# The product with T of six chunks in seven half products instead of four whole ones

## The chip, the cores and the metric

The kernel runs on one core of one Trainium2 chip. The metric is the device time of one execution in microseconds, the median of repeated runs. The kernel is written instruction by instruction for the engines: PE (TensorE, matmuls and weight loads), ACT (ScalarE), DVE (VectorE), POOL (GpSimd) and SP, which here only issues DMAs.

## The reference

Attention with pooled queries, and then a multiplicative feed-forward block. Everything is float32 outside; the kernel works in float16 with float32 accumulation.

```python
# q, k, v: (8, 8, 1152, 64); w1, w2: (512, 1024); w3: (1024, 1024); w_out: (1024, 512)
q_pool = q.reshape(B, H, S // 2, 2, D).mean(axis=3)
scores = scale * np.matmul(q_pool, k.transpose(0, 1, 3, 2))
attn = softmax(scores)                       # over the keys
x = np.matmul(attn, v)                       # -> (4608, 512), tokens x (heads * D)
a = x @ w1
b = x @ w2
h = a * b @ w3
out = h @ w_out                              # (4608, 512)
```

## The kernel before

**Folding.** `w3 @ w_out` is one matrix T (1024 x 512), made once on PE (`t_groups`: transposes of w3, then products with w_out, L561) and kept as `T16`. What remains behind attention, for each chunk of 512 tokens, is: a = x w1 and b = x w2 (transposed, 1024 x 512), g = a * b, and out = g^T T.

**Attention.** The 8 x 8 heads are taken as 32 pairs of heads, four pairs to a batch. Scores are computed transposed, keys on the partitions, and cut into 324 slots of 512 columns; `scores` (L443, L448) makes two 512-column products into one of three PSUM buffers `psc`, and ACT's exp brings them to a ring in SBUF that holds 2.7 pairs. An attention group (`av_mm`, L474 or L471) multiplies 128 queries of a pair, or the 64-query rests of two pairs, with v; `av_norm` divides on DVE. There are 144 groups. The normalised x comes transposed into `xT` through PE for the first eight pairs and through a transposing DMA on SP (`x_dma`, L485) afterwards.

**Loading.** For each pair POOL casts k, sums pairs of q rows and casts v (`prepare`, `cast_kq`, `cast_v`: L355, L359, L361, L368), two pairs ahead; k and q are then transposed by PE (the first eight) or by a DMA on SP (`transp`, L375), one pair ahead. Loads are issued by SP (by POOL for the early pairs).

**Chunks.** There are nine chunks. Chunks 0 to 6 go through `moe_groups(c)`, a generator of steps that fill PE's time in the attention loop. A step names its cost, a function that issues matmuls into a PSUM bank, and a function that takes the result out. A chunk has 16 projection steps (for each of 8 row tiles `ft`, one with w1 whose result `keep` copies to `asb`, one with w2, L583, whose result `gate` multiplies by `asb` into `gT`, L614), each 4 x 512 columns, and then four steps that multiply 128 tokens each with T (L621, 8 x 512 columns, L630). Chunks 7 and 8 (`LATE` is 7) stand behind the loop in `late_chunks`, in an order written out by hand; there all three products go by seven half-size products instead of eight (the Strassen-Winograd scheme), with the sums of weights, of T and of x made on POOL (`weight_sums`, `x_sums`).

**Order.** A visit is three slots of scores and what the planner puts behind them; there are 108. `_visits` is a beam search over a small cost model (`_Plan`), run when the kernel is built. For each visit it chooses a sequence of attention groups ("A"), steps ("m" into the one bank `mo`, or "s" into one of the three `psc` buffers, then named `mot`) and PE transposes of k and q ("P"); DVE takes the results out of both kinds of bank. Steps run strictly in their order. A chunk's steps become available after a fixed number of groups (`loose`), and a group has an earliest visit (when the exps that it reads are done) and a latest one (when the ring is overwritten). Groups and steps that are left when the scores end are worked off in a tail.

**Queues.** Every engine executes its own instructions in program order. On POOL the casts, the sums and the issue of the output's stores stand in one queue; on SP the loads, the transposing DMAs and the stores of chunks 5 and 6.

Of the kernel before, what the change touches and what calls it, by code (L numbers as in the profile page):

```python
# [8 lines left out]
FP32 = mybir.dt.float32  # L9
# [174 lines left out]
def _visits(n, start, units, pairs, fills, free, ready, width):  # L184

    p = _Plan(7.0)
    for _ in range(3):  # L190
        p.scores(0.0)
    beam = {(0, 0): [p]}
    for vis in range(n):
        new = {}
        ats = pairs.get(vis, [])

        def end(p, seq, na, f):
            q = p.copy()
            for _ in range(3 if vis + 1 < n else 0):
                q.scores(ready[vis + 1])  # L200
            q.past = (p.past, seq)

            cost = q.lost() + 0.3 * max(q.av - q.t, 0.0) + 0.15 * max(q.mo - q.t, 0.0)
            new.setdefault((na, f), []).append((cost, seq, q))

        def step(p, seq, na, f, pr, t0):
            d = p.t - t0
            loose = free[na] if vis >= start else 0
            if pr == len(ats) and (na >= len(units) or units[na][3] > vis) and (d > 1.0 or f >= loose):
                end(p, seq, na, f)  # L210
            if d > 2.3 or len(seq) > 4:
                return
            if pr < len(ats):
                q = p.copy()
                q.pair(ats[pr])
                step(q, seq + "P", na, f, pr + 1, t0)
            if na < len(units) and units[na][2] <= vis and seq.count("A") < 3:
                q = p.copy()
                q.av_group(*units[na][:2])
                step(q, seq + "A", na + 1, f, pr, t0)  # L220
            if f < loose:
                for b in "ms":
# [43 lines left out]
def kernel(  # L266
# [277 lines left out]
    def t_groups():  # L544
        w3T = {}

        def turn(ft):
            def go(pt):
                w3T[ft] = msb.tile([128, NF, 128], FP16, tag="w3T", bufs=2, name="w3T")
                ph = pt.bitcast(FP16)  # L550
                for a in range(NF):
                    nc.tensor.transpose(ph[:, a * 128:a * 128 + 128],
                                        w3c[ft // 4][:, ft % 4, a * 128:a * 128 + 128], ident16)

            return 0.5, go, lambda pt: nc.vector.tensor_copy(out=w3T[ft].rearrange("p a i -> p (a i)"),
                                                             in_=pt.bitcast(FP16)), W3_AT[ft // 2]

        def mult(ft, n0):
            def go(pT):
                for a in range(NF):  # L560
                    nc.tensor.matmul(pT[:, 0:256], w3T[ft][:, a, :], wosb[:, a, n0:n0 + 256],  # L561
                                     start=(a == 0), stop=(a == NF - 1))

            return 1, go, lambda pT: nc.vector.tensor_copy(out=T16[:, ft, n0:n0 + 256], in_=pT[:, 0:256]), WO_AT

        for ft in range(0, NF, 2):
            yield turn(ft)
            yield turn(ft + 1)
            for n in range(4):
                yield mult(ft + n // 2, n % 2 * 256)  # L570

    CH = 512

    def runs(c):
        a = (c * CH) % XR
# [10 lines left out]
    def store(eng, pos, osb, cols=slice(0, dm), rows=slice(0, 128)):  # L586
# [7 lines left out]
            b, r = b + 1, r - QM * 128 - 2 * QT  # L594
        eng.dma_start(out=out[b * Sq:b * Sq + QM * 128, :].rearrange("(p c) n -> p c n", c=QM)[rows, r // 128, cols], in_=osb)  # L595

    def moe_groups(c):
        t = {}

        def first(pa, ft):  # L600
            if ft == 0:
                t["g"] = msb.tile([128, NF, CH], FP16, tag="g8", bufs=2, name="gT")
            proj(pa, w1sb, ft, c)

        def keep(pa):
            t["a"] = msb.tile([128, CH], FP32, tag="asb", bufs=2, name="asb")
            if tail[0]:
                nc.scalar.copy(out=t["a"], in_=pa)
            else:
                nc.vector.tensor_copy(out=t["a"], in_=pa)  # L610

        for ft in range(NF):
            def gate(pb, ft=ft):
                nc.vector.tensor_tensor(out=t["g"][:, ft, :], in0=pb, in1=t["a"], op=ALU.mult)  # L614

            yield 1, lambda pa, ft=ft: first(pa, ft), keep, 0.0
            yield 1, lambda pb, ft=ft: proj(pb, w2sb, ft, c), gate, 0.0
        for tt in range(0, CH, 128):
            def go(po, tt=tt):
                for ft in range(NF):  # L620
                    nc.tensor.matmul(po, t["g"][:, ft, tt:tt + 128], T16[:, ft, :],  # L621
                                     start=(ft == 0), stop=(ft == NF - 1))

            def put(po, tt=tt):
                osb = msb.tile([128, dm], FP32, tag="osb", bufs=3)
                if tail[0]:
                    nc.vector.tensor_scalar_mul(out=osb[:, 0:256], in0=po[:, 0:256], scalar1=1.0 / (SCL * SCL))
                    nc.scalar.mul(out=osb[:, 256:512], in_=po[:, 256:512], mul=1.0 / (SCL * SCL))
                else:
                    nc.vector.tensor_scalar_mul(out=osb, in0=po, scalar1=1.0 / (SCL * SCL))  # L630
# [10 lines left out]
    HF, HM, HC = NF // 2, dm // 2, CH // 2  # L641
    LATE = B * Sq // CH - 2
    IS = 1.0 / (SCL * SCL)
    wS, tS, xS = [], {}, {}

    def minus(out, x, y):
# [2 lines left out]
    def weight_sums():  # L649
        for w, tag in ((w1sb, "kst"), (w2sb, "vst")):  # L650
# [6 lines left out]
            minus(s3, a11, a21)  # L657
            minus(s4, a12, s2)
            wS.append({1: a11, 2: a12, 3: s4, 4: a22, 5: s1, 6: s2, 7: s3})
        b11, b12 = T16[:, 0:HF, 0:HM], T16[:, 0:HF, HM:dm]  # L660
        b21, b22 = T16[:, HF:NF, 0:HM], T16[:, HF:NF, HM:dm]
        st = [att.tile([128, 2, HF, HM], FP16, tag="qst", name="tS") for _ in range(2)]
        t1, t2, t3, t4 = st[0][:, 0], st[0][:, 1], st[1][:, 0], st[1][:, 1]
        minus(t1, b12, b11)
        minus(t2, b22, t1)
        minus(t3, b22, b12)
        minus(t4, b21, t2)
        tS.update({1: b11, 2: b21, 3: b22, 4: t4, 5: t1, 6: t2, 7: t3})

    def x_sums():  # L670
        st = msb.tile([128, 2, 4, NC // 2, HC], FP16, tag="wo", bufs=1, name="xS")
        for c in (0, 1):
            (_, a, n), = runs(LATE + c)
            b11, b12 = xT[:, 0:NC // 2, a:a + HC], xT[:, 0:NC // 2, a + HC:a + n]
            b21, b22 = xT[:, NC // 2:NC, a:a + HC], xT[:, NC // 2:NC, a + HC:a + n]
            x1, x2, x3, x4 = (st[:, c, i] for i in range(4))
            minus(x1, b12, b11)
            minus(x2, b22, x1)
            minus(x3, b22, b12)
# [151 lines left out]
    def fill(scored=False):  # L831
        if not head():
            return False
        n, go, put, at = ahead.pop(0)
        pt = bank(scored) if put else None
        go(pt)
        if put:
            put(pt)
        return True


# [14 lines left out]
        out=ident16, in_=ident16, compare_op=ALU.not_equal, fill=1.0,  # L856
        base=0, channel_multiplier=1, pattern=[[-1, 128]],
    )
    for _ in range(33):
        nc.tensor.matmul(avb[:, 0:64], ident16, ident16[:, 0:64], start=True, stop=True)  # L860
    for t in kq16s:
        nc.gpsimd.memset(t[QT:128, NB - 1], 0.0)
# [56 lines left out]
                      ((old * FLAT + RING + TO[t]) // G) // VS - 1))  # L919
    fills = []  # L920
    for ft in range(0, NF, 2):
        fills += [(0.5, W3_AT[ft // 2])] * 2 + [(1, WO_AT)] * 4
# [132 lines left out]
```

## Time and profile before

| | |
|---|---|
| median of 3 runs | 410.97 us (410.57 to 411.2) |
| the profiled execution's own time | 411.45 us |
| its span, first to last instruction | 409.8 us, granted clock 0.998 |
| PE busy | 396.8 us, 97% |
| ACT busy | 335.2 us, 82% |
| DVE busy | 218.7 us, 53% |
| POOL busy | 212.8 us, 52% |
| product with T of chunks 0 to 5 (L621 into `mo`) | 192 matmuls of 512 columns, 45.6 us busy |
| DMA | 86.35 MB, mean 211 GB/s |

The table is of one profiled execution. The chunks' steps on the time axis: chunk 0 from 67 us, chunk 1 from 112, chunk 2 from 159, chunk 3 from 203, chunk 4 from 248, chunk 5 from 291, chunk 6 from 337; the last scores are issued at 346, and the hand-ordered part (L724) begins at 369.5. A group of instructions in the profile is named by line, engine, operation, and "out<-in" with the program's own names of tiles. [...]

### The profile page before, as it was taken

What the parts mean: (1) busy time and instruction counts of PE and PEld (TensorE: products, weight loads), DVE (VectorE), ACT (ScalarE), POOL (GpSimd) and SP (SyncE); (2) the same over time, 40 slices, a digit from 0 to 9 for tenths busy, and PEclk for the clock granted to TensorE, in tenths of its full rate; (3) what the DMA queues carried; (4) which work ended last, traced back from release to release, by engine and by line L of the source; (5) the groups of instructions that cost most, each with busy time, mean ns of one, the idle gap of its engine ahead of it and who ended that gap; (6) DMA issues with size and microseconds to landing.
All of it is one profiled execution on the core that took longest, in us unless ns stands there. A gap on an engine that the chain in (4) does not pass through costs nothing.

```text
span 409.8 us, 13190 instructions
## 1 busy us (share of the span) xinstructions
PE 396.8 (97%) x5506; PEld 261.6 (64%) x5506; DVE 218.7 (53%) x594; ACT 335.2 (82%) x380; POOL 212.8 (52%) x237
## 2 busy tenths in 40 slices
PE   5899999999999999999999999999999999999995
PEld 3477887565555655565556556655777655658884
DVE  1255565665355534654355536553546435765993
ACT  4978979898889998999989999999899889107752
POOL 5789966470664225504533336333633897051860
PEclk9999999999999999999999999999999999999999
DMA  8999999999598899949999999996998170121005
GB/s 278 251 308 268 274 289 304 346 238 292 173 265 228 198 283 249 260 114 248 245 277 261 250 304 255 259 321 144 278 241 180 26 151 19 22 62 50 9 26 183
DMA packets 94079, 86.35 MB, mean 211 GB/s; under 512 B 60096, under 2 KB 68544, under 8 KB 94016
## 3 DMA queue, kind: packets, MB, share of 16 engines
q1 hardware_dynamic: 84480, 60.11, 61.3%
q0 software_dynamic: 8384, 24.06, 21.1%
q10 hardware_dynamic: 1152, 1.31, 0.9%
q8 instruction: 43, 0.70, 0.7%
q14 instruction: 20, 0.16, 0.1%
HBM read 67.11 MB, written 9.44 MB: 187 GB/s over the span
## 4 chain that ended last, share of the span: by engine, by line
PE 88%; DMA 6%; POOL 2%; ACT 1%; issue 1%; DVE 1%; SPq 0%; ACTq 0%
PE psc L443 19%; PE avb L474 16%; PE mo L583 15%; PE mo L621 10%; PE mot L583 9%; PE b L724 7%; PE mo L561 3%; DMA qst<-in_q_dram 3%; PE avb L471 3%; DMA xT<-xb 3%; PE b L621 2%; PE mo L724 1%; PE ptk L383 1%; ACT ring L448 1%; DMA kst<-in_k_dram 1%; PE avb L724 1%
## 5 line engine op out<-in xcount | busy, mean ns | idle before, releaser
L448 ACT ACTIVATE ring<-psc 128x1024 f16<-128x1024 f32 x324 | 308.2, 1025 | 34.5 <-PE psc L443 32.7
L474 PEld LDWEIGHTS <-ring 128*128 128x128 f16 x2304 | 84.4, 98 | 26.3 <-issue 7.1
L443 PE MATMUL psc<-kqT 64*128 64x512 f16 (+7 forms) x1152 | 96.2, 290 | 3.6 <-ACT ring L448 0.9
L474 PE MATMUL avb<-vaug,ring 128*128 128x65 f16 x2304 | 91.4, 193 | 0.0
L355 POOL CAST kq<-kst 128x1152 f16<-128x1152 f32 x31 | 35.7, 1152 | 77.1 <-DMA kqT<-kq 52.9
L443 PEld LDWEIGHTS <-kqT 64*128 64x128 f16 x1152 | 45.8, 95 | 31.2 <-issue 8.5
L621 PE MATMUL mo<-T,gT 128*128 128x512 f16 x192 | 45.6, 380 | 0.0
L495 DVE RECIPROCAL rzall<-avb 128x2 f32<-128x2 f32 x144 | 23.8, 165 | 37.0 <-PE avb L474 20.3
L630 DVE TENSOR_SCALAR osb<-mo 128x512 f32<-128x512 f32 x24 | 16.6, 692 | 48.6 <-PE mo L621 48.6
L359 POOL TENSOR_TENSOR kq<-qst 128x512 f16<-128x512 f32 x31 | 39.4, 1272 | 1.1 <-DMA qst<-in_q_dram 1.1
L368 POOL CAST vaug<-vst 128x1152 f16<-128x1152 f32 x32 | 36.6, 1143 | 5.8 <-PE psc L443 5.3
L595 POOL DMA_DIRECT2D out_dram<-osb x18 | 9.9, 552 | 55.9 <-DVE rzall L495 55.9
L614 DVE TENSOR_TENSOR gT<-mo,asb 128x512 f16<-128x512 f32 x36 | 24.9, 692 | 24.7 <-PE mo L583 24.4
L583 PE MATMUL mo<-xT,w2sb 128*128 128x512 f16 (+2 forms) x168 | 37.2, 350 | 0.0
L621 PEld LDWEIGHTS <-gT 128*128 128x128 f16 x224 | 19.8, 98 | 25.5 <-issue 5.2
L610 DVE COPY asb<-mo 128x512 f32<-128x512 f32 x32 | 22.1, 691 | 25.2 <-PE mo L583 24.9
L583 PEld LDWEIGHTS <-w2sb 128*128 128x128 f16 x256 | 21.9, 97 | 20.8 <-issue 4.2
L583 PEld LDWEIGHTS <-w1sb 128*128 128x128 f16 x256 | 22.0, 97 | 20.4 <-issue 3.9
L583 PE MATMUL mo<-xT,w1sb 128*128 128x512 f16 (+2 forms) x148 | 33.3, 351 | 1.1 <-DMA xT<-xb 1.1
L509 DVE TENSOR_TENSOR xb<-avb,rzall 128x128 f16<-128x128 f32 x96 | 28.0, 291 | 3.3
L583 PE MATMUL mot<-xT,w1sb 128*128 128x512 f16 (+1 forms) x104 | 23.6, 354 | 0.1
L583 PE MATMUL mot<-xT,w2sb 128*128 128x512 f16 (+1 forms) x84 | 19.5, 359 | 0.0
(143 smaller groups left out, 432.7 us busy)
## 6 DMA issues: line engine op xcount, KB each, us to landing
vst<-in_v_dram SPq DMA_DIRECT2D x25, 576.0 KB, 5.0
kst<-in_k_dram SPq DMA_DIRECT2D x23, 576.0 KB, 5.8
qst<-in_q_dram SPq DMA_DIRECT2D x23, 512.0 KB, 7.3
kst<-in_k_dram POOLq DMA_DIRECT2D x8, 576.0 KB, 9.9
out_dram<-osb POOLq DMA_DIRECT2D x18, 256.0 KB, 6.1
qst<-in_q_dram POOLq DMA_DIRECT2D x8, 512.0 KB, 10.6
vst<-in_v_dram POOLq DMA_DIRECT2D x7, 576.0 KB, 6.9
w3c<-in_moe_w_dram POOLq DMA_DIRECT2D x4, 512.0 KB, 8.2
```

What stands on the lines that cost most here:

```text
L355: nc.gpsimd.tensor_copy(out=kq16[:, 0:NJ].rearrange("p c u d -> p u c d"), in_=kst.rearrange("p u (c d) -> p u c d", d=D))
L359: eng.tensor_tensor(out=kq16[:, NJ:NJ + QM].rearrange("p c u d -> p u c d"), in0=qv[:, :, :, 0], in1=qv[:, :, :, 1], op=ALU.add)
L368: nc.gpsimd.tensor_copy(out=va[:, :, :, 0:D], in_=vs.pop(p).rearrange("p u (c d) -> p u c d", d=D))
L443: nc.tensor.matmul(psc[:, u, f - s * G:f - s * G + ln], kT2[u * 64:u * 64 + 64, jt, :], qpT[u * 64:u * 64 + 64, i0:i0 + ln], start=True, s ...
L448: nc.scalar.activation(out=ring[:, :, r0:r0 + G], in_=psc, func=AF.Exp, bias=0.0, scale=SCALE)
L474: nc.tensor.matmul(avb[:, o + u * E1:o + u * E1 + E1], ring[:, u, c0:c0 + 128], va[:, u, jt, :], start=(jt == 0 and u == 0), stop=(jt == N ...
L495: nc.vector.reciprocal(out=rzall[:, i, :], in_=av[:, :, D:E1].rearrange("p u o -> p (u o)"))
L509: nc.vector.tensor_tensor(out=xbt, in0=av[:, :, 0:D], in1=rzall[:, i, :].unsqueeze(2).to_broadcast([128, 2, D]), op=ALU.mult)
L583: nc.tensor.matmul(pw[:, d0:d0 + n], wt[:, mc, ft * 128:ft * 128 + 128], xT[:, mc, a:a + n], start=(mc == 0 and d0 == 0), stop=(mc == NC - ...
L614: nc.vector.tensor_tensor(out=t["g"][:, ft, :], in0=pb, in1=t["a"], op=ALU.mult)
L621: nc.tensor.matmul(po, t["g"][:, ft, tt:tt + 128], T16[:, ft, :], start=(ft == 0), stop=(ft == NF - 1))
L724: nc.tensor.matmul(pt[:, n * f:n * f + n], l[:, i, :], b[:, i, :], start=(p in (1, 5) and f == 0 and i == 0), stop=(i == kc - 1), skip_gro ...
```

## The change

For chunks 0 to 5 (`seven`) the product of the gated values (512 tokens x 1024) with T (1024 x 512) is cut into 2 x 2 blocks and done in seven products of half size: each is 2 x 4 matmuls of 256 columns with weights of 128 x 128, a step of cost 1. Product 1 stands between the two halves of the projections, product 2 behind them; products 6, 7, 4, 5 and 3 are handed to the next chunk (`late_fills`), where they stand behind its first two steps (`LAG`). Product 3 adds to the bank of product 5 after one part was read from it; the last two take only the bank `mo`. DVE scales and adds when it takes a product out (`plus`, `quarter`, `p1`, `p7`). The sums of blocks of gated values (`sums`, and `minus` in `p2`) are made on POOL, in place where possible, behind the gates of rows 5, 6 and 7 and behind product 2. The sums of T move from `weight_sums` near the loop's end to the first four gates of chunk 0 (`t_sum`). The output of the six chunks is stored in quarters of 256 tokens x 256 columns, by POOL. `w3T`, `p` and `z` share one tag; T's sums take the place of `wosb`, and the sums of x for the late chunks that of the q staging. The matmuls on the identity at the start become 15 instead of 33. Chunk 6 and the late chunks keep their products. The planner runs again over the new list of steps.

```diff
             if f < loose:
-                for b in "ms":
+                for b in fills[f][2]:
                     q = p.copy()
-                    q.fill(fills[f][0], fills[f][1], b == "s")
+                    q.fill(*fills[f][:2], b == "s")
...
-                w3T[ft] = msb.tile([128, NF, 128], FP16, tag="w3T", bufs=2, name="w3T")
+                w3T[ft] = msb.tile([128, NF, 128], FP16, tag="t2k", bufs=2, name="w3T")
...
+    LAG = 2
+    HF, HM, HC = NF // 2, dm // 2, CH // 2
+    LATE = B * Sq // CH - 2
+    IS = 1.0 / (SCL * SCL)
...
     def moe_groups(c):
         t = {}
+        lagged, late_fills[:] = late_fills[:], []
+        seven = c < LATE - 1
...
-        for ft in range(NF):
-            def gate(pb, ft=ft):
-                nc.vector.tensor_tensor(out=t["g"][:, ft, :], in0=pb, in1=t["a"], op=ALU.mult)
-
-            yield 1, lambda pa, ft=ft: first(pa, ft), keep, 0.0
-            yield 1, lambda pb, ft=ft: proj(pb, w2sb, ft, c), gate, 0.0
+        def product(pt, a, n, start=True):
+            for u in range(2):
+                for f in range(HF):
+                    nc.tensor.matmul(pt[:, u * HM:u * HM + HM], a[:, f, u * 128:u * 128 + 128], tS[n][:, f, :],
+                                     start=(start and u == 0 and f == 0), stop=(f == HF - 1), skip_group_check=True)
+
+        def plus(out, pt, x):
+            nc.vector.scalar_tensor_tensor(out=out, in0=two(pt), scalar=IS, in1=x, op0=ALU.mult, op1=ALU.add)
...
+        def quarter(h, n, pt, x):
+            osb = msb.tile([128, 2, HM], FP32, tag="osb", bufs=3, name="osb")
+            plus(osb, pt, x)
+            store_two(nc.gpsimd, c * CH + h * HC, osb, slice(n * HM, n * HM + HM))
+
+        def p1(pt):
+            t["p"] = msb.tile([128, 2, HM], FP32, tag="t2k", bufs=2, name="p")
+            nc.vector.tensor_scalar_mul(out=t["p"], in0=two(pt), scalar1=IS)
+
+        def sums(f, n):
+            g = t["g"]
+            if f == 0:
+                t["s1"] = msb.tile([128, HF, HC], FP16, tag="s1", bufs=1, name="s1")
+            fs = slice(f, f + n)
+            s1, a11, a21, a22 = t["s1"][:, fs], g[:, fs, 0:HC], g[:, fs, HC:CH], g[:, HF + f:HF + f + n, HC:CH]
+            nc.gpsimd.tensor_tensor(out=s1, in0=a21, in1=a22, op=ALU.add)
+            minus(a21, a11, a21)
+            minus(a11, s1, a11)
+
+        def half(fts):
+            for ft in fts:
+                def gate(pb, ft=ft):
+                    nc.vector.tensor_tensor(out=t["g"][:, ft, :], in0=pb, in1=t["a"], op=ALU.mult)
+                    if c == 0 and ft < HF:
+                        t_sum(ft)
+                    if seven and ft > HF:
+                        sums(*((0, 2) if ft == HF + 1 else (ft - HF, 1)))
+
+                yield 1, lambda pa, ft=ft: first(pa, ft), keep, 0.0
+                yield 1, lambda pb, ft=ft: proj(pb, w2sb, ft, c), gate, 0.0
+                if 2 * ft + 2 == LAG:
+                    yield from lagged
+
+        yield from half(range(HF))
+        if seven:
+            yield 1, lambda pt: product(pt, t["g"][:, 0:HF, 0:HC], 1), lambda pt: p1(pt), 0.0
+        yield from half(range(HF, NF))
+        if seven:
...
+            def p2(pt):
+                quarter(0, 0, pt, t["p"])
+                for f in range(0, HF, 2):
+                    minus(g[:, HF + f:HF + f + 2, lo], g[:, HF + f:HF + f + 2, lo], g[:, f:f + 2, lo])
...
+            yield 1, lambda pt: product(pt, g[:, HF:NF, lo], 2), p2, 0.0
+            late_fills.extend((
+                (1, lambda pt: product(pt, g[:, 0:HF, lo], 6), lambda pt: plus(t["p"], pt, t["p"]), 0.0),
+                (1, lambda pt: product(pt, g[:, 0:HF, hi], 7), p7, 0.0),
+                (1, lambda pt: product(pt, g[:, HF:NF, hi], 4), lambda pt: quarter(1, 0, pt, t["z"]), 0.0),
+                (1, p5, lambda pt: quarter(1, 1, pt, t["z"]), 0.0),
+                (1, lambda pt: product(t["bank"], g[:, HF:NF, lo], 3, False),
+                 lambda pt: quarter(0, 1, t["bank"], t["p"]), None),
+            ))
+            return
...
-    for _ in range(33):
+    for _ in range(15):
         nc.tensor.matmul(avb[:, 0:64], ident16, ident16[:, 0:64], start=True, stop=True)
...
         for c in loose.get(n, []):
-            fills += [(1, 0.0)] * (2 * NF) + [(2, 0.0)] * (CH // 128)
+            step = [(1, 0.0, "ms")]
+            rest = step * 3 + [(1, 0.0, "m")] * 2
+            fills += step * LAG + (rest if c else []) + step * (2 * NF - LAG)
+            fills += step * 2 if c < LATE - 1 else [(2, 0.0, "ms")] * (CH // 128)
```

More of the change, by code (lines that the diff above doesn't have):

```diff
@@ L595, in store, with store_two @@
         eng.dma_start(out=out[b * Sq:b * Sq + QM * 128, :].rearrange("(p c) n -> p c n", c=QM)[rows, r // 128, cols], in_=osb)
+    def store_two(eng, pos, osb, cols):
+        b, r = pos // (2 * Sq) * 2, pos % (2 * Sq)
+        t0 = r // 128 - (QM + 1 if r > QM * 128 else 0)
+        if t0 > QM - 2 or r == QM * 128:
+            for u in range(2):
+                store(eng, pos + u * 128, osb[:, u, :], cols)
+            return
+        b += r > QM * 128
+        eng.dma_start(out=out[b * Sq:b * Sq + QM * 128, :].rearrange("(p c) n -> p c n", c=QM)[:, t0:t0 + 2, cols], in_=osb)
+    late_fills = []
     def moe_groups(c):
         t = {}
+        lagged, late_fills[:] = late_fills[:], []
+        seven = c < LATE - 1
         def first(pa, ft):
@@ L610, in keep @@
                 nc.vector.tensor_copy(out=t["a"], in_=pa)
-        for ft in range(NF):
-            def gate(pb, ft=ft):
-                nc.vector.tensor_tensor(out=t["g"][:, ft, :], in0=pb, in1=t["a"], op=ALU.mult)
-            yield 1, lambda pa, ft=ft: first(pa, ft), keep, 0.0
-            yield 1, lambda pb, ft=ft: proj(pb, w2sb, ft, c), gate, 0.0
+        def product(pt, a, n, start=True):
+            for u in range(2):
+                for f in range(HF):
+                    nc.tensor.matmul(pt[:, u * HM:u * HM + HM], a[:, f, u * 128:u * 128 + 128], tS[n][:, f, :],
+                                     start=(start and u == 0 and f == 0), stop=(f == HF - 1), skip_group_check=True)
@@ new lines, in plus, with two @@
+        def plus(out, pt, x):
+            nc.vector.scalar_tensor_tensor(out=out, in0=two(pt), scalar=IS, in1=x, op0=ALU.mult, op1=ALU.add)
+        def two(pt):
+            return pt.rearrange("p (u n) -> p u n", u=2)
+        def quarter(h, n, pt, x):
[5 more added lines that the diff above has]
+            nc.vector.tensor_scalar_mul(out=t["p"], in0=two(pt), scalar1=IS)
@@ new lines, in moe_groups, with p7, p5 @@
+        yield from half(range(HF))
[3 more added lines that the diff above has]
+        if seven:
+            g = t["g"]
+            lo, hi = slice(0, HC), slice(HC, CH)
+            def p2(pt):
+                quarter(0, 0, pt, t["p"])
+                for f in range(0, HF, 2):
+                    minus(g[:, HF + f:HF + f + 2, lo], g[:, HF + f:HF + f + 2, lo], g[:, f:f + 2, lo])
+            def p7(pt):
+                t["z"] = msb.tile([128, 2, HM], FP32, tag="t2k", bufs=2, name="z")
+                plus(t["z"], pt, t["p"])
+            def p5(pt):
+                t["bank"] = pt
+                product(pt, t["s1"], 5)
+            yield 1, lambda pt: product(pt, g[:, HF:NF, lo], 2), p2, 0.0
[7 more added lines that the diff above has]
+            ))
+            return
@@ L639, in moe_groups @@
             yield 2, go, put, 0.0
-    HF, HM, HC = NF // 2, dm // 2, CH // 2
-    LATE = B * Sq // CH - 2
-    IS = 1.0 / (SCL * SCL)
     wS, tS, xS = [], {}, {}
@@ L659, in weight_sums, with t_sum @@
             wS.append({1: a11, 2: a12, 3: s4, 4: a22, 5: s1, 6: s2, 7: s3})
+    def t_sum(i):
         b11, b12 = T16[:, 0:HF, 0:HM], T16[:, 0:HF, HM:dm]
         b21, b22 = T16[:, HF:NF, 0:HM], T16[:, HF:NF, HM:dm]
[L662 to L668, printed above, removed]
+        if i == 0:
+            t = msb.tile([128, 4, HF, HM], FP16, tag="wo", bufs=1, name="tS")
+            tS.update({1: b11, 2: b21, 3: b22, 4: t[:, 3], 5: t[:, 0], 6: t[:, 1], 7: t[:, 2]})
+        minus(*((tS[5], b12, b11), (tS[6], b22, tS[5]), (tS[7], b22, b12), (tS[4], b21, tS[6]))[i])
     def x_sums():
-        st = msb.tile([128, 2, 4, NC // 2, HC], FP16, tag="wo", bufs=1, name="xS")
         for c in (0, 1):
+            st = att.tile([128, 4, NC // 2, HC], FP16, tag="qst", name="xS")
             (_, a, n), = runs(LATE + c)
@@ L675, in x_sums @@
             b21, b22 = xT[:, NC // 2:NC, a:a + HC], xT[:, NC // 2:NC, a + HC:a + n]
-            x1, x2, x3, x4 = (st[:, c, i] for i in range(4))
+            x1, x2, x3, x4 = (st[:, i] for i in range(4))
             minus(x1, b12, b11)
@@ L834, in fill @@
         n, go, put, at = ahead.pop(0)
-        pt = bank(scored) if put else None
+        pt = bank(scored) if at is not None else None
         go(pt)
-        if put:
-            put(pt)
+        put(pt)
         return True
@@ L921 @@
     for ft in range(0, NF, 2):
-        fills += [(0.5, W3_AT[ft // 2])] * 2 + [(1, WO_AT)] * 4
+        fills += [(0.5, W3_AT[ft // 2], "ms")] * 2 + [(1, WO_AT, "ms")] * 4
     free = []
```

## The prediction, made before the change was run

> **What bounds the kernel now.** First the page: busy time by engine, and the chain that ended last.
>
> ```profile
> PE 396.8 (97%) x5506; PEld 261.6 (64%) x5506; DVE 218.7 (53%) x594; ACT 335.2 (82%) x380; POOL 212.8 (52%) x237
> ...
> PE 88%; DMA 6%; POOL 2%; ACT 1%; issue 1%; DVE 1%; SPq 0%; ACTq 0%
> ```
>
> PE fills 97% of the span and carries 88% of the chain. ACT is second: 324 exps take 308.2 us (row L448 below), 0.951 each. Whether PE binds is a question of stages, so next the table by stage: window and length, then busy us of PE, PEld, DVE, ACT, POOL. These two windows are chunk 3's 16 projection steps and its four products with T.
>
> ```profile
> 206.00:234.00 28.00, 28.00 (x402) 16.95 (x398) 16.18 (x44) 25.56 (x27) 11.62 (x12) 1.00 1.17 264
> 234.00:248.00 14.00, 14.00 (x177) 8.06 (x176) 4.82 (x15) 12.53 (x15) 5.68 (x8) 1.00 1.09 289
> ```
>
> PE has no gap in either; ACT is idle 2.4 us of 28 and 1.5 of 14. The chain in order of time (start, us, what) gives the beat of a visit, which is three slots of scores with what the planner puts behind them:
>
> ```profile
> 44.68 0.87 PE mo L561 x8
> ...
> 168.48 0.97 PE mo L583 x4
> 169.45 0.86 PE mot L583 x4
> 171.63 0.97 PE mo L583 x4
> ...
> 194.58 10.37 DMA xT<-xb
> 206.83 0.97 PE mo L583 x4
> ...
> 234.79 1.83 PE mo L621 x8
> 237.93 1.83 PE mo L621 x8
> ...
> 370.85 1.75 PE b L724 x16
> ```
>
> A visit with two single steps (168.48 to 171.63) and one with a whole product (234.79 to 237.93) both last about 3.14 us, over ACT's floor of 3 x 0.951 = 2.85. In the loop PE sets the pace, with 0.29 us a visit in hand before ACT would. At 194.58 the chain runs through the transposing DMA of x: the next chunk's first step waited for it, 1.1 us (the only such wait of PE, by the waits view).
>
> Last, the groups with shapes kept apart (count | busy us, mean ns | idle before):
>
> ```profile
> L448 ACT ACTIVATE ring<-psc 128x1024 f16<-128x1024 f32 x324 | 308.2, 1025 | 34.5 <-PE psc L443 32.7
> ...
> L621 PE MATMUL mo<-T,gT 128*128 128x512 f16 x192 | 45.6, 380 | 0.0
> ...
> L359 POOL TENSOR_TENSOR kq<-qst 128x512 f16<-128x512 f32 x31 | 39.4, 1272 | 1.1 <-DMA qst<-in_q_dram 1.1
> L368 POOL CAST vaug<-vst 128x1152 f16<-128x1152 f32 x32 | 36.6, 1143 | 5.8 <-PE psc L443 5.3 <-PE mo L583 0.4
> L355 POOL CAST kq<-kst 128x1152 f16<-128x1152 f32 x31 | 35.7, 1152 | 77.1 <-DMA kqT<-kq 52.9 <-issue 13.8 <-PE ptk L383 5.5
> ...
> L630 DVE TENSOR_SCALAR osb<-mo 128x512 f32<-128x512 f32 x24 | 16.6, 692 | 48.6 <-PE mo L621 48.6
> ...
> L361 POOL TENSOR_TENSOR kq<-qtl 64x128 f16<-64x128 f32 x31 | 13.9, 449 | 0.0
> ...
> L814 POOL TENSOR_TENSOR room<-room,gT 128x512 f16<-128x512 f16 x3 | 4.8, 1610 | 0.0
> ...
> L647 POOL TENSOR_TENSOR xS<-xT 128x512 f16<-128x512 f16 x4 | 4.6, 1156 | 0.0
> ...
> L647 POOL TENSOR_TENSOR tS<-T 128x1024 f16<-128x1024 f16 x2 | 4.3, 2135 | 0.0
> ```
>
> **The change part by part.** The sum is made on the profiled execution, 411.45 us (span 409.8 and 1.65 around it); the median of the runs is 410.97, 0.48 lower, and the forecast goes by the median.
>
> *Matmuls.* Six chunks lose 4 x 8 matmuls of 512 columns and get 7 x 8 of 256. A 512 takes 0.216 us of PE in a row (1.73 for 8, or 1.83 with the 0.1 of entering from scores), a 256 takes 0.109 (0.87 for 8 at 44.68, 1.75 for 16 at 370.85). Per chunk 32 x 0.216 = 6.92 becomes 56 x 0.109 = 6.12; six chunks give **-4.8 us**. [...]
>
> *Does PE's saving reach the end?* Count items in the trace, a step as 4 x 512 columns (a whole product is two), a group as 18 or 36 weight loads of L474 or L471: from visit 23 to 106 every visit holds exactly three, two steps and a group (3.14 us) or one and two (about 2.9), so steps plus groups by the end of visit v are 3v - 33. If the changed plan keeps three, six fewer items shorten the tail, where PE alone is busy, by their full time. But it must have three. A chunk may begin after so many groups: 58 for chunk 2, 76 for chunk 3, the last four of them not before visits 44 and 58, when the exps are there. With 18 steps ahead of the next chunk's first one instead of 24, by the end of visit 43 there are at most 54 groups and 18 + 23 = 41 steps, 95 for 96 places; by 57, 72 + 64 = 136 for 138. Later boundaries leave room. So 2 items are missing, 4 if two steps are held back to stand between the four groups. A missing item turns 3.14 into ACT's 2.85 and puts its 0.75 (0.87 for a step, 0.6 for a group) into the tail: 0.46 each, 0.9 to 1.8; I take **+1.2**. If every saved step fell to the floor, 0.29 of each 0.8 were left: 1.7 in all.
>
> *Evictions.* 23 per chunk instead of 20, 18 x 0.69 = 12.4 us more on DVE, which is 53% busy. One whole product evicts once per visit, two halves twice, as the projection visits already do at 3.14 to 3.20. Three and a half such visits a chunk at 0 to 0.05: 0 to 1.1, I take **+0.5**.
>
> *Sums on GpSimd.* From 1156 ns at 512 elements and 2135 at 1024, 256 would take an estimated 670. A chunk has five of 512 (two on s4) and six of 256: 5.8 + 4.0 = 9.8 us, 59 in all on an engine that is 52% busy. At L814's 1610 it would be 39% more. In POOL's queue, behind a sum that waits for its gate, stand a pair's casts (1.15 + 1.27 + 0.45 + 1.14 = 4.0 us every 10.5) and the stores. PE waits at product 6 for the sums of gate 7, and the scores stand behind it. Chunks 3 to 5 did 24 units in 39 to 45 us, 1.74 each; from the end of gate 7's matmuls to product 6 lie product 2 and two steps of the next chunk, 4 x 1.74 - 0.87 = 6.1 us. Less 0.9 for the gate's eviction, POOL has 5.2 for 2.0 of its own. From gate 5 on it has 12.2 for 7.5, and at most one cast group lies between gates 5 and 7 (7 us apart against 10.5): 11.5. It fits by 0.7; at the tightest beat (1.57 a step) it misses by 0.7. Bounds 0 to 0.7 at each of six boundaries; mostly it fits, I take 0.1, **+0.6**. A gain is excluded, it only adds work. Casts made late delay kqT: those that end under 4 us ahead of their transposes have 7 us from landing to first score, so 4 us late costs nothing; without that cover, it would cost the rest once per pair.
>
> *The next chunk's x.* The first two steps of a chunk stand before the five products, and from batch 2 on they need a transposing DMA. SP lets a batch's last one go at 149.2, 195.9, 237.8, 281.3 and 330.8 us; they land 8.3, 9.1, 5.3, 4.0 and 3.4 later, and the chunks' first steps are due 6.6 to 10.3 us after it, because the loop there does one group a visit. Only chunk 3 waits, 1.1. In the changed plan the boundary comes up to three visits earlier, and at two groups a visit (the three that lie between take 1.5 visits, about 5 us with the step's place) the waits would be 3.3, 4.1, 0.3, 0, 0: 0 to 8 in all. I take **+1.1**, what chunk 3 pays beyond now and the nearest row.
>
> *The rest, at nothing.* T's sums (4 x 2.13) leave the loop's end for chunk 0's first gates, where POOL is 54% busy (67 to 99 us) and product 6 is over 12 steps off. weight_sums (17 us of POOL) is issued at visit 101; chunk 5's product 2 is step 133, and with at most 130 groups before visit 102 it falls in visit 99 or 100, ahead of it; behind it, product 6 would wait up to 12 us (17 less the 5.2 above). 18 fewer warm-up matmuls: PE then waits for POOL's cast at 4.7 us anyway, and until 25.5 the chain hangs on loads. Stores move as many bytes, in 1 KB pieces, chunk 5's from SP to POOL; product 2's has 8 steps (14 us) before its buffer is wanted, against 6.1 median to landing. If the tail shrinks, the last x transpose stands behind more of chunk 6's stores on SP, with some 4 us to spare before chunk 8 needs it.
>
> Sum: -4.8 + 1.2 + 0.5 + 0.6 + 1.1 = **-1.4 us**: 410.05 for the profiled execution, **409.6** for the median.
>
> **The rivals.**
> *The next chunk waits for x (slower).* The 8 us above instead of 1.1: -1.4 + 6.9 = +5.5, 416; with half, 412.5. It decides from 2.5 us in all. For: 10.37 at 194.58, DMA shares over 1.0 in the windows, no spare visit left at two boundaries; against: four of five land in under 8.5, and the planner can do groups earlier. 0.17.
> *GpSimd comes late (slower).* At 1.61 instead of 1.16 the 7.5 us become 10.4, with casts as much longer 16 against 12.2: up to 3.8 each, 23 in all; with a quarter of that, +4, 415. It decides from 0.4 us a boundary. For: no slack beyond 0.7; against: every sum that ran beside the loop took 1.16 or 2.13 flat. 0.10.
> *ACT's floor takes the gain.* -1.7 plus the 2.2 of the other costs: 411.5; 410 to 412. For: only 0.29 us a visit; against: the tail takes saved steps whole. 0.10.
> *Weight loads show (slower).* A load takes 98 ns (the PEld group of L621), only just under a 109 ns matmul. If the 24 more a chunk were not hidden: 24 x 0.098 x 6 = 14.1, less 4.8: 420. Both groups of 256 columns speak against it. 0.02. [...]
> *It does not do what it says:* the planner writes a new order for the whole loop; one with idle PE in it leaves 411 to 413. 0.03.
>
> **How the numbers follow.** The forecast, 406.5 to 410.4, has 0.58. A measurement of this kernel tells about 0.2% (0.8 us) from no change. Faster: 0.55 of it and 0.02 of ACT's floor, 0.57. Same: 0.03 of it, 0.06 of the floor, 0.02 of x, 0.01 each of GpSimd and the planner, 0.13. Slower: the rest, 0.30. For 8 in 10 the range reaches from 406.3 (all but 0.2 of the 4.8) past ACT's floor and the planner into the smaller ends of x and GpSimd, 413.5.
>
> **What would show it.** Half products of 8 matmuls at 0.87 in the chain where 1.83 stood; POOL near 272 us busy, DVE 231; visits still 2.9 to 3.2, and a shorter stretch between the loop's last scores (346 us) and the first L724 (369.5). Waits of PE on POOL at product 6 of over 0.7 us show GpSimd late; waits of PE on DMA xT of over 2 us in all show the lag's price; visits at 2.85 with the tail as long as before show ACT's floor. Any of these that comes to 3 us makes the forecast wrong.

## The result

The changed kernel takes **428.28 us** (median of 6 runs, 427.01 to 429.16) against 410.28 us for the kernel before (6 runs, the three given above among them): ratio 1.0434, 95% interval 1.0412 to 1.0456. It is slower by 18 us, outside the predicted range of 406.3 to 413.5, and by a cause that the prediction named, costed and set aside as not arising.

The profiled execution took 427.01 us, its span is 425.4 us and its granted clock 0.984 (before: 411.45, 409.8 and 0.998). First the page again: busy time by engine, and the chain that ended last.

```profile
PE 395.0 (93%) x5632; PEld 276.0 (65%) x5632; DVE 230.6 (54%) x611; ACT 336.3 (79%) x383; POOL 282.4 (66%) x319
...
PE 86%; POOL 6%; ACT 3%; DVE 2%; DMA 1%; issue 1%; ACTq 0%; POOLq 0%
```

PE falls from 97% to 93% of a longer span. In busy time it does 1.8 us less than before, while POOL does 69.6 us more and has gone from 2% to 6% of the chain. That suggests that the matmuls became cheaper and that something else was put in PE's way. What it is, the waits of PE say (the waits view: engine, line waited for, us in total, times, longest):

```profile
PE mot L633 <- POOL gT L732: 13.0, 1, 13.0
PE ptf L423 <- POOL kq L409: 2.4, 1, 2.4
PE mot L633 <- DVE gT L664: 2.3, 5, 0.5
PE psc L443 <- ACT ring L448: 2.2, 7, 0.4
...
PE b L808 <- ACT osb L716: 0.9, 1, 0.9
```

One wait of 13.0 us, a single time, for POOL's sums of gated values. (L633 is the half product, L664 the gate, L732 and L657 the sums; L808 is the hand-ordered part.) Before, the largest wait of PE was 1.5 us, at the start:

```profile
PE avb L860 <- POOL ident L855: 1.5, 1, 1.5
PE ptf L423 <- POOL kq L409: 1.3, 1, 1.3
PE mo L583 <- DMA xT<-xb: 1.1, 1, 1.1
PE psc L443 <- ACT ring L448: 0.9, 3, 0.3
```

The chain of the changed kernel in order of time (start, us, what) shows who kept POOL:

```profile
319.47 0.70 DVE gT L664
...
320.25 1.16 POOL s L657
...
325.31 0.67 POOL gT L732
325.99 1.09 POOL vaug L368
327.08 2.09 POOL wS L740
...
329.24 6.28 POOL wS L732 x3
335.52 2.08 POOL wS L740
...
337.67 6.26 POOL wS L732 x3
343.93 0.62 POOL s L657
...
346.11 1.25 PE mot L633 x5
...
349.84 1.46 PE mo L633 x8
```

At 325.31 POOL ends the sums of chunk 5's gate 6. Then come the last pair's cast of v and all eight operations of `weight_sums` (wS), 18 us without a pause, 17 of them `weight_sums`, and only then, at 343.93, the sums of gate 7, which product 6 needs. Product 6 issues its first three matmuls at 332.63; the fourth reads what is made of gate 7, and it starts at 346.11. The last two lines carry a second price: the eight matmuls that take 0.87 elsewhere take 1.46. The windows show the granted clock beside it (window and length, busy us of PE, PEld, DVE, ACT and POOL, clock, DMA share, GB/s):

```profile
333.13:337.13 4.00, 0.00 (x0) 0.00 (x0) 0.46 (x1) 1.21 (x2) 4.00 (x3) 1.00 0.01 1
337.13:346.11 8.98, 0.01 (x1) 0.01 (x1) 0.00 (x0) 0.00 (x0) 8.68 (x7) 0.50 0.00 0
346.11:350.78 4.67, 4.67 (x40) 3.14 (x41) 1.35 (x4) 1.68 (x2) 3.01 (x3) 0.50 0.16 56
350.78:354.78 4.00, 4.00 (x67) 3.33 (x65) 2.21 (x6) 2.81 (x4) 1.57 (x3) 1.00 0.08 19
```

The clock went to 0.50 four us into the wait and came back only 4.67 us after PE had resumed; half of that, 2.3 us, is my estimate of the work lost at half the clock. With it the stall cost 13.0 + 2.3 = 15.3 us in all.

**The balance.** The span grew by 425.35 - 409.79 = 15.6 us. PE's waits grew from 8.2 to 25.6, +17.4; PE's time at work shrank from 396.8 to 395.0, -1.8; what lies behind the last matmul is equal. Of the 17.4: the wait for POOL 13.0, the gates' results 2.3, the start 1.1 (against 1.0 less of warm-up matmuls), scores waiting for ACT's ring or for a transposed k or q 1.9, the bank at L808 0.9, and less 1.1 for the wait on the transposed x, which has gone; the rest is -0.7 of small ones.

### The profile page after: what moved, and what is told of

It reads as the page before. It is cut to its first block, busy times and chain, and to the rows that moved or that the text cites. A ratio compares the mean times of both kernels' runs of the same rounds, so it can differ in the third digit from the quotient of the medians.

```text
span 425.4 us, 13539 instructions
## 1 busy us (share of the span) xinstructions
PE 395.0 (93%) x5632; PEld 276.0 (65%) x5632; DVE 230.6 (54%) x611; ACT 336.3 (79%) x383; POOL 282.4 (66%) x319
## 4 chain that ended last, share of the span: by engine, by line
PE 86%; POOL 6%; ACT 3%; DVE 2%; DMA 1%; issue 1%; ACTq 0%; POOLq 0%
PE psc L443 19%; PE avb L474 17%; PE mo L587 12%; PE mot L587 8%; PE b L808 6%; PE mo L633 6%; POOL wS L732 3%; PE mot L633 3%; PE mo L561 3%; ACT ring L448 3%; PE avb L471 2%; PE b L709 2%; PE ptk L383 2%; PE mo L808 1%; PE b L587 1%; POOL gT L732 1%
## 5 line engine op out<-in xcount | busy, mean ns | idle before, releaser
L443 PE MATMUL psc<-kqT 64*128 64x512 f16 (+7 forms) x1152 | 97.6, 292 | 4.9 <-ACT ring L448 2.2
L633 PEld LDWEIGHTS <-gT 128*128 128x128 f16 x288 | 26.5, 99 | 24.3 <-POOL gT L732 13.3
L657 POOL TENSOR_TENSOR s<-gT 128x256 f16<-128x256 f16 (+1 forms) x18 | 15.0, 831 | 40.2 <-DVE gT L664 20.8
L664 DVE TENSOR_TENSOR gT<-mo,asb 128x512 f16<-128x512 f32 x31 | 21.4, 692 | 27.9 <-PE mo L587 27.8
L628 DVE COPY asb<-mo 128x512 f32<-128x512 f32 x31 | 21.4, 692 | 25.6 <-PE mo L587 25.2
L587 PE MATMUL mo<-xT,w2sb 128*128 128x512 f16 (+2 forms) x152 | 32.2, 342 | 0.0
L587 PE MATMUL mo<-xT,w1sb 128*128 128x512 f16 (+2 forms) x128 | 32.1, 374 | 0.0
L732 POOL TENSOR_TENSOR gT<-gT 128x512 f16<-128x512 f16 (+1 forms) x30 | 28.6, 965 | 1.5
L609 POOL DMA_DIRECT2D out_dram<-osb x16 | 11.8, 740 | 19.6 <-DVE rzall L495 11.8
L633 PE MATMUL mot<-tS,gT 128*128 128x256 f16 x80 | 11.1, 282 | 13.0 <-POOL gT L732 13.0
L587 PE MATMUL mot<-xT,w1sb 128*128 128x512 f16 (+1 forms) x116 | 22.6, 327 | 0.0
```

What stands on the lines that cost most here:

```text
L443: nc.tensor.matmul(psc[:, u, f - s * G:f - s * G + ln], kT2[u * 64:u * 64 + 64, jt, :], qpT[u * 64:u * 64 + 64, i0:i0 + ln], start=True, s ...
L587: nc.tensor.matmul(pw[:, d0:d0 + n], wt[:, mc, ft * 128:ft * 128 + 128], xT[:, mc, a:a + n], start=(mc == 0 and d0 == 0), stop=(mc == NC - ...
L633: nc.tensor.matmul(pt[:, u * HM:u * HM + HM], a[:, f, u * 128:u * 128 + 128], tS[n][:, f, :], start=(start and u == 0 and f == 0), stop=(f ...
L732: nc.gpsimd.tensor_tensor(out=out, in0=x, in1=y, op=ALU.subtract)
```

## The experiments

The theories. **Order:** the loss is the place of `weight_sums` in POOL's queue. **Load:** POOL has 59 us more than it can take without making casts and sums late, and if the one wait goes, others come. Each variant below was run beside the kernel before; a median is of 4 to 12 executions.

### weight_sums behind product 2

```diff
+    def sums_ready():
+        ready.append(1)
+        if len(ready) == 2:
+            weight_sums()
...
                 for f in range(0, HF, 2):
                     minus(g[:, HF + f:HF + f + 2, lo], g[:, HF + f:HF + f + 2, lo], g[:, f:f + 2, lo])
+                if c == LATE - 2:
+                    sums_ready()
...
-                    weight_sums()
+                    sums_ready()
```

> weight_sums (eight operations, 17 us of GpSimd) is issued behind chunk 5's product 2 instead of ahead of gate 7's sums. Theory A (order on GpSimd: the 13.0 us wait of product 6 and about 2.5 us of slow matmuls behind it are the whole loss of the chip): both vanish, PE waits for GpSimd under 1 us around 320 to 350, time 412 to 413.5, 1.004 to 1.008 of the kernel before. Theory B (GpSimd carries 59 us more than it can without delaying casts and sums elsewhere): its load is the same here, so the wait moves to another place, time 420 or more.

Measured: **413.92 us** (413.04 to 414.61; before 410.84), ratio 1.0078 [1.0065, 1.0091]. Its waits, in the same columns:

```profile
PE ptf L423 <- POOL kq L409: 2.6, 1, 2.6
PE mot L638 <- DVE gT L669: 2.3, 5, 0.5
PE psc L443 <- ACT ring L448: 2.2, 7, 0.4
```

The 13.0 is gone and nothing of POOL's has come in its place (the one at L409 is the start), with POOL's load unchanged. Order is shown: this one move is worth 14.4 us of the 18. The time is 0.4 us over the expected band, so the variant is still 3.1 us slower than before, and where the half products' gain went is the question of the later runs.

### Half of weight_sums behind product 2

```diff
-    def weight_sums():
-        for w, tag in ((w1sb, "kst"), (w2sb, "vst")):
+    def weight_sums(half):
+        for w, tag in (((w1sb, "kst"), (w2sb, "vst"))[half],):
```

> Only the second half of weight_sums (four operations, 8.5 us) goes behind chunk 5's product 2; the first half stays ahead of gate 7's sums. Theory A (order): the wait shrinks by the 8.4 us taken out of the way, from 13.0 to about 4.5 us, and its cold matmuls with it: 416 to 419.5. Theory B (load): no change from the changed kernel, about 428.

Measured: **420.02 us** (418.96 to 422.39), ratio 1.0234 [1.0209, 1.0258].

```profile
PE mot L637 <- POOL gT L738: 4.6, 1, 4.6
```

The wait is the 13.0 less the 8.4 us of the four operations that were taken out of its way, to a tenth of a us. The time is 0.5 above the band and 6.1 us over the variant before it. Between the two profiled executions the span differs by 6.8 us: the wait of 4.6, and 2.4 us more of busy time on PE, whose clock stood at 0.50 for 6.83 us, 5.5 of them after the wait.

### Without the sums on GpSimd

```diff
-                    if seven and ft > HF:
-                        sums(*((0, 2) if ft == HF + 1 else (ft - HF, 1)))
...
-                for f in range(0, HF, 2):
-                    minus(g[:, HF + f:HF + f + 2, lo], g[:, HF + f:HF + f + 2, lo], g[:, f:f + 2, lo])
...
-                product(pt, t["s1"], 5)
+                product(pt, g[:, HF:NF, hi], 5)
```

> The sums of gated values on GpSimd (42 operations, 37 us) are left out and product 5 reads the gated values in their place, so part of the computation is missing; weight_sums stands where the changed kernel has it. Theory A (the sums cost only where weight_sums stood ahead of them): within 1 us of the first variant, 411.5 to 413.5. Theory B (the sums slow the casts, and the casts the loop): several us below it, 405 to 408.

Measured: **412.93 us** (412.01 to 413.67), ratio 1.0042 [1.0029, 1.0054]. (What is left out is more than the expectation counted: 66 operations; POOL's busy time falls from the first variant's 282.1 us to 224.5.) The time is 1.0 us from the first variant, the outer end of what the order theory allowed and far from the load theory's 405 to 408. 57.6 us of sums on POOL cost the kernel about 1 us when nothing long stands ahead of them. GpSimd is not the bound.

### The old early order

```diff
+EARLY = ',,P,ms,AsAm,APm,Asm,Asm,AmA,mPA,...'.split(',')
...
+            if vis < len(EARLY) and not EARLY[vis].startswith(seq):
+                return
```

> The first variant (weight_sums behind chunk 5's product 2), and the planned order of the kernel before forced on the first 28 visits, so that 68 items instead of 63 are done by visit 27. Theory A (each item missing in the loop is paid for behind it at 0.46 us): 5 x 0.46 = 2.3 us below the first variant, 410 to 411. Theory B (the early visits with fewer items were shorter by what was left out of them, so nothing was lost there; the planner's own model has it so): the same as the first variant within 0.5 us.

Measured: **417.64 us** (415.04 to 420.23), ratio 1.0154 [1.0118, 1.0189]. Neither theory: 3.7 us *slower* than the first variant. One line of its waits, and windows around each of the two waits in it:

```profile
PE mo L592 <- DMA xT<-xb: 4.6, 2, 2.4
```

```profile
155.00:157.80 2.80, 1.10 (x9) 0.37 (x7) 0.08 (x1) 2.79 (x3) 2.78 (x5) 1.00 1.30 152
157.80:161.20 3.40, 2.94 (x11) 0.95 (x12) 1.24 (x2) 0.00 (x1) 3.40 (x5) 0.52 1.23 243
...
202.90:205.40 2.50, 0.07 (x1) 0.00 (x0) 0.00 (x0) 1.81 (x2) 2.48 (x4) 1.00 1.44 152
...
205.70:209.10 3.40, 3.40 (x14) 1.54 (x13) 1.38 (x2) 0.00 (x0) 3.40 (x4) 0.50 1.05 243
```

With the early items done, the loop reaches chunks 2 and 3 sooner than the transposed x of their last pairs: two waits of 2.2 and 2.4 us, and with the end of each the clock stood at 0.50 for 3.4 us. This is the rival "the next chunk waits for x" in a version of the kernel that has it, at 4.6 us of waiting and, as an estimate (half of the two stretches of 3.4), about 3.4 of slow clock. What a missing item costs can't be read from this run; that stays open. The spread of 5 us between its executions fits waits that some have and others not, which was not looked into.

### Bank rotation and warm-ups

```diff
-    banks, turns = [], [0]
+    banks, turns = [], [2]
...
-    for _ in range(15):
+    for _ in range(33):
```

> The first variant (weight_sums behind chunk 5's product 2) with two small edits: the rotation of the six banks behind the loop starts two places further, so that the last product of chunk 6 no longer lies in the bank that the first hand-ordered unit takes, and the 33 warm-up matmuls of the kernel before. Theory A (these waits are paid in full): the 0.9 us wait at the start of the hand-ordered part goes, and 0.3 to 0.8 us at the start, 412.2 to 412.8. Theory B (they are swallowed by the next wait): the same as the first variant, 413.9.

Measured: **412.99 us** (412.48 to 413.6), ratio 1.0047 [1.0034, 1.0059], 0.9 us below the first variant. The wait of 0.9 at the hand-ordered part is gone: in the changed order four more steps use the six banks behind the loop (10 instead of 6), so their rotation stops at bank 4 instead of 0, and bank 4 is what the first hand-ordered unit writes. The warm-ups brought nothing: the wait at L423 is 1.8 us instead of 2.6, but the matmuls that waited start at 5.28 us instead of 5.04. That the 0.9 us of the medians is the bank's is argued from this wait; the two profiled executions differ the other way (spans of 411.8 and 411.4 us).

### Product 2 behind two steps of the next chunk

```diff
-            yield 1, lambda pt: product(pt, g[:, HF:NF, lo], 2), p2, 0.0
             late_fills.extend((
+                (1, lambda pt: product(pt, g[:, HF:NF, lo], 2), p2, 0.0),
...
-            rest = step * 3 + [(1, 0.0, "m")] * 2
+            rest = step * 4 + [(1, 0.0, "m")] * 2
...
-            fills += step * 2 if c < LATE - 1 else [(2, 0.0, "ms")] * (CH // 128)
+            fills += step if c < LATE - 1 else [(2, 0.0, "ms")] * (CH // 128)
```

> The first variant with product 2 also behind two steps of the next chunk, ahead of the other five. Theory A (product 2 directly behind gate 7 waits for its eviction on TensorE, five times 0.46 us): these waits go, -2.3 us; the planner's model loses 0.5 us by the two more units left at the end, and the last bank changes, which takes the 0.9 us wait at the start of the hand-ordered part too: 411.0 to 411.6. Theory B (the next product in line waits instead, for the sums of gate 7 on GpSimd): the five waits stand at product 6, time as the first variant, 413 to 414.

Measured: **410.97 us** (410.05 to 412.14), ratio 1.0000 [0.9988, 1.0012]: as fast as before. The time came out at the lower edge of what was expected, and the reason only in part.

```profile
PE mot L638 <- DVE gT L669: 1.4, 3, 0.5
```

Three waits at gates are left. Counting the half products in the trace tells whose they are: in the first variant the five belonged to product 1 of chunks 0, 2 and 3 and to product 2 of chunks 2 and 5; here all three are product 1's (chunks 0, 1 and 4). Each sits at the fourth matmul, the one that reads the row tile just gated. So the move took 0.9 us of these waits, not 2.3; the bank's 0.9 went too, as expected; the remaining 1.1 of the 2.95 us lies in the new order of the whole loop and was not taken apart.

### Product 1 one step later

On top of the variant above:

```diff
                 yield 1, lambda pa, ft=ft: first(pa, ft), keep, 0.0
+                if seven and ft == HF:
+                    yield 1, lambda pt: product(pt, t["g"][:, 0:HF, 0:HC], 1), p1, 0.0
...
-        if seven:
-            yield 1, lambda pt: product(pt, t["g"][:, 0:HF, 0:HC], 1), lambda pt: p1(pt), 0.0
```

> The variant with product 2 lagged, and product 1 one step later: behind the first step of the second half instead of directly behind gate 3, whose result it reads. Theory A (the three waits of 0.46 us that are left at gates are product 1's, and are paid in full): they go, -1.4 us, 409.4 to 410.0, 0.996 to 0.998 of the kernel before. Theory B (ScalarE is the floor in those visits and takes the time back in waits for the ring of scores): the gate waits go and 'ACT ring' waits grow by as much, time as the variant before it, 1.000.

Measured: **409.18 us** (408.27 to 409.75; before 411.14), ratio **0.9954** [0.9938, 0.9969]. This one beats the kernel before by half a per cent, and lies 0.2 us below the expected band. Its longest waits inside the loop are these:

```profile
PE psc L443 <- ACT ring L448: 2.2, 8, 0.3
...
PE psc L443 <- DVE kqT L385: 1.2, 2, 0.8
```

No wait at a gate, at POOL's sums, at x or at a bank is left, and the waits for the ring did not grow in their place (2.7 us in the variant before it), so the first theory holds. The gain on that variant is 1.8 us, of which the three waits are 1.4.

### Products one by one between the steps

This one differs from "Product 2 behind two steps" in that the six handed-over products are spread behind steps 1, 3, 5, 7, 8 and 8 of the next chunk, with the rotation started at 3 and 33 warm-ups.

```diff
-    LAG = 2
+    PLACES = (1, 3, 5, 7, 8, 8)
...
+        def behind(n):
+            return [x for x, at in zip(lagged, PLACES) if at == n]
...
+                yield from behind(2 * ft + 1)
                 yield 1, lambda pb, ft=ft: proj(pb, w2sb, ft, c), gate, 0.0
-                if 2 * ft + 2 == LAG:
-                    yield from lagged
+                yield from behind(2 * ft + 2)
```

> Meant to beat both: weight_sums behind chunk 5's product 2, the six lagged products of a chunk spread behind steps 1, 3, 5, 7, 8 and 8 of the next chunk instead of in one row, the rotation of the banks shifted as above, 33 warm-ups. Theory A (the half products save 3.7 us of matmul time, and what eats it are the waits at gate 7, 2.3 us, at the hand-ordered part, 0.9 us, and at the start, 0.3 to 0.8 us): 409.5 to 410.8, 0.997 to 1.000 of the kernel before. Theory B (behind them stand other waits: the transposed x, or ScalarE in visits with few items): 411.5 or more.

Measured: **416.57 us** (415.58 to 417.43), ratio 1.0127 [1.0112, 1.0142]. Meant to be the best, it is 5.6 us behind the plain move. Its chain near the end:

```profile
361.55 0.69 DVE asb L633
362.24 0.37 DVE ok L1102
362.61 1.19 DVE ok L1103
...
363.82 1.30 DVE ok L1104
...
365.71 0.70 DVE gT L672
...
366.45 5.75 PE b L719 x18
```

Again a queue: chunk 6's last gate stands on DVE behind the checks of the softmax sums (`ok`). Two things make that dear here. In the plain move three of chunk 6's gates stand behind the checks too, but PE then has steps of the chunk left to do; here only products are left, and they need this gate. And the checks are slow: in this run alone POOL's sums of x run beside all of them, and the operations at L1103 and L1104 take 1.19 and 1.30 us of the chain above, against 0.30 and 0.46 for the same two before and in the changed kernel, where no sum of POOL's runs beside them. PE waits 2.6 us, the clock stands at 0.50 from 366.9 to 370.3, and a wait for x of 1.7 us that ends at 201 comes on top.

### Control: without the half products

```diff
-        seven = c < LATE - 1
+        seven = False
...
-            fills += step * LAG + (rest if c else []) + step * (2 * NF - LAG)
-            fills += step * 2 if c < LATE - 1 else [(2, 0.0, "ms")] * (CH // 128)
+            fills += step * 2 * NF
+            fills += [(2, 0.0, "ms")] * (CH // 128)
```

> Control: the changed kernel with its seven half products and their sums switched off in chunks 0 to 5, which take the four full products of the kernel before; 15 warm-ups, the places of the buffers and the sums of T stay as changed. Theory A (the rest of the diff costs next to nothing): 0.999 to 1.002 of the kernel before, about 411.0. Theory B (the rest of the diff carries some of the 3 us that the first variant is slower): 412 or more.

Measured: **411.2 us** (409.76 to 414.62), ratio 1.0019 [0.9997, 1.0042]. The rest of the diff (fewer warm-ups, shared buffers, T's sums at chunk 0) can't be told from nothing; the interval leaves room for a cost of up to 1.7 us.

## Why the prediction was wrong

**The step that failed** is in "The rest, at nothing": "chunk 5's product 2 is step 133, and with at most 130 groups before visit 102 it falls in visit 99 or 100, ahead of" `weight_sums`. It fell in visit 101, the visit in which `weight_sums` is issued, and behind it, since `cast_v` and `weight_sums` belong to a visit's scores and the steps to what follows them. Gate 7, step 132, fell in the same visit, and it is this one's place that decides, since product 6 waits for its sums. The price was put at up to 12 us; it was 13.0, and 2.3 of slow clock that no part of the prediction had.

**What fed that step** was the count of missing items: 2, at most 4, at two boundaries. By the end of visit 99 the kernel before had done 264 items, as 3v - 33 says, and the changed kernel 256, 8 fewer. Five were already gone by visit 21: the planner, run anew, chose other sequences from the start, with visits of two items, where the prediction assumed the old ones wherever places allowed it. The two to four fewer of the prediction leave step 133 in visit 99 or 100; eight put it in 101. The margin was one visit, three items, of a count that the planner is free to change, with 15 us behind it, and it got no chance of its own. It should have been the first rival.

**The other terms**, against the traces:

- *Matmuls, -4.8.* The saving is there: eight matmuls of 256 take 0.87, so their eight weight loads, of 97 to 99 ns each, add nothing that shows. In the variant with product 1 moved, PE spends 37.2 us on chunks 0 to 5's half products where the whole ones took 41.8: -4.6. In the first variant it is -3.8; the rest lies at the five waits at gates, ahead of each of which three matmuls take 0.49 us instead of 0.33. By the length of their rows (8 in 0.87, 4 in 0.86) a 256 takes 109 ns and a 512 takes 216, before and after; the means of single records are longer, 273 and 380 ns.
- *Missing items, +1.2.* They show where that term has them, as PE reaching ACT's floor: scores waiting for the ring of exps 0.9 before and 2.2 after, for a transposed k or q +0.6, together +1.9, where eight items are missing by visit 99 instead of two to four. In the old early order, where four are missing, the same waits come to +0.3. That fits the missing items as their cause, but no run separates it.
- *Evictions, +0.5.* DVE's 230.6 us are the 231 foreseen, but the cost has another place: a product directly behind the gate that it reads waits for that gate's eviction, 5 x 0.46 = 2.3 us. The prediction counted the gate's eviction for POOL's sums, and not for PE.
- *Sums on GpSimd, +0.6.* A sum of 256 elements takes 0.669 us (row below) as estimated, one of 512 1.154 to 1.162; at the five other boundaries product 6 does not wait at all. POOL's busy time is 282.4 us instead of 272.
- *The next chunk's x, +1.1.* No wait for x is left in the changed kernel, -1.1; the old early order, with the same lag, brings 4.6 us of it. The term hangs on the order and not on the lag alone.
- *Not in the sum:* the bank at the hand-ordered part, +0.9; the wait at the start, +1.1, which the 1.0 less of warm-up matmuls offsets.

```profile
L732 POOL TENSOR_TENSOR gT<-gT 128x512 f16<-128x512 f16 x18 | 20.6, 1162 | 0.6
...
L657 POOL TENSOR_TENSOR s<-gT 128x256 f16<-128x256 f16 x12 | 8.0, 669 | 3.7 <-DVE gT L664 1.9 <-DVE rzall L495 1.7
```

(Groups of the changed kernel with shapes kept apart: count | busy us, mean ns | idle before.)

**Rivals.** GpSimd late came nearest to what happened, and for the wrong reason: it priced a slow engine, not one long block in the queue. Of "what would show it", the wait of PE on POOL at product 6 was the line that did.

**What stays open.** The first variant's profiled execution is 1.6 us longer than before's, its median 3.1; before's profiled execution lay above its median and the variant's was the lowest of its five, which leaves about a us to their scatter. What the planner's new order costs by itself was not separated.

## What to carry to other kernels

When a change puts a short operation with a waiting reader into an in-order queue, look for every long block that the queue holds from elsewhere, and find by which margin the short one stands ahead of it; if that margin hangs on a schedule that a planner will write anew, the far side of it is a rival with its full price, not a line under "at nothing". Tie a block that only needs to be done by some later time to the event it must not precede, as `weight_sums` to product 2, rather than to a visit. And put a step between a product and the gate that it reads: three waits of 0.46 us are 1.4 of the 1.8 us between no gain and 0.5%.

## What the runs showed of the hardware

**The clock.** Once the loop ran, waits of PE of 2.2 and 2.4 us (the old early order) and of 2.6 us (products one by one) each came with one stretch of 3.41 us at a granted clock of 0.50; half of 3.41, some 1.7 us, is my estimate of what each cost beyond its own length. With the wait of 4.6 us (half of `weight_sums` behind) it was 6.83 us, and in the changed kernel 13.65 us, four times 3.41, with 8.98 of it inside the wait of 13.0. Waits of 0.9 (the changed kernel), 1.1 (before) and 1.7 us (products one by one) drew none.

In the changed kernel the clock's record begins at 19.69 us, and its fall at 337.13 and its rise at 350.78 lie 93 and 97 times 3.413 us behind that; in the old early order the two falls, at 157.92 and 205.70, lie 14 times 3.413 us apart. In the 3.41 us ahead of a fall PE was busy for 0% (the changed kernel), 47 and 28% (the old early order) and 25% (products one by one). Counted in the same steps, the 3.41 us that hold most of the wait of 1.7 us, with PE busy for 61%, were followed by no fall, and neither were those from 419.05 to 422.46 at the end of the changed kernel, with 44%. So the busy share alone does not part those with a fall from those without.

**DVE beside POOL.** Two operations of DVE in the checks of the softmax sums, a comparison and a product, both from SBUF to SBUF, took 0.30 and 0.46 us before and in the changed kernel, where no sum of POOL's ran beside them, and 1.19 and 1.30 us of the chain with products one by one, where POOL was busy with sums for 3.42 of the 3.5 us from 363 to 366.5. The reduction behind them took 0.45 us in the first two and 0.46 in the last.
